# Clustered attention and a maxout FFN: small operations on other engines, weight chains by threes, other weight layout, new order

## The chip, the cores and the metric

The kernel runs on one core of a Trainium2 chip. A core has a matrix engine (TensorE, PE in the profile, with its weight loads as PEld), VectorE (DVE), ScalarE (ACT), GpSimd (POOL) and SyncE (SP), which here only issues DMA. Each engine works through its own list of instructions in order and waits on semaphores for the others. The metric is the device time of one execution in microseconds.

## The reference

Four batches, eight heads, 768 tokens, 64 values per head, 16 centroids per head. Each query and each key goes to the centroid with which its cosine is largest, and a query sees only keys of its own cluster:

```python
mask = q_assign[:, :, :, None] == k_assign[:, :, None, :]
scores = np.where(mask, scale * q @ k.T, -1e9)
attn = exp(scores - max(scores)) ; attn /= sum(attn) + 1e-9
x = (attn @ v), heads side by side            # 3072 x 512
h = max(max(x @ w1, x @ w2), x @ w3)          # 3072 x 768
out = h @ w_out                               # 3072 x 512
```

All inputs and the output are float32.

## The kernel before

*Precision.* TensorE works mostly on pairs of float16 values: each float32 operand is scaled by a power of two and split into a high half and a low half (what the high half leaves), and a product is three float16 products. The power of two comes from a maximum over the tile (L736, L738 for queries and keys), a little matmul that spreads the maxima over the partitions (L754, L407), and a few operations on one or two columns.

*Preparation* (`prep`). Heads go in pairs, four pairs per batch. For each pair the transposed queries and keys are loaded (L730; pair 0 to 3 of batch 0 share four buffers, so the loads of pair 2 wait until pair 0's two tiles have been read by the low-half operation L809), scaled and split, multiplied with the centroids (`cluster_raw`, L787 and L796 in batch 0, on float32), and the winning cluster is turned into one-hot rows ("mask rows") that are added to the contraction of the score matmuls, so that keys of other clusters come out far below. The first pair of batch 0 is "fast": its copies between partition halves (L852) and its four mask rows (L653) are done by compute engines and not by DMA.

*Attention* (`visit`, `tile_units`). A visit is one batch, one pair and one half of the queries: six score tiles of 128 queries by 768 keys, in time order 192 steps. Each tile: score matmuls into PSUM (L1288, L1290; three large PSUM buffers in all), a scaling with the maximum (L1299, VectorE), the exponential with its sum (L1305, ScalarE). From batch 1 on ("norm") the sum is scaled (L1325) and inverted (L1326) on VectorE, and the tile is multiplied with it while it is split (L1363 or L1361, then high half L375 to L377, then low half L1311 or L1372). On even steps from 24 on the exponentials stay in their PSUM buffer until the low half is taken. Tiles are transposed by TensorE (L1336) in the even steps below 40 and in the first pass of batch 0, by DMA (L1314) otherwise. At the end of a visit the product with the values (L1225 or L1236) gives a part of x.

*Weights* (`weights`, `piece`, `split16`). Each of 18 input weight pieces (w1, w2, w3 by six blocks of 128 columns) is loaded (L1032), converted from float32 bits by a cast (L1037 or L1039) and a shift-and-or (L1043), scaled and split. The six row blocks of w_out go the same way, and each has a chain of its own on VectorE: row maximum (L1107), floor, cut to a power of two, reciprocal, factor.

*FFN* (`ffn`). For each of eight groups of 384 tokens 18 hidden products (L1453, twelve matmuls each), their maximum in PSUM evictions (L1467), a split, and three output products (L1508, eighteen matmuls each), an eviction (L375 or L377) and a store (L1522).

*What sets the order.* The kernel is a list of "units" (one operation each, with what it depends on and the buffers it leases), numbered as they are added. `ORDER` says in which order they are emitted, and so each engine's program order; `HANDS` gives, for each unit that several engines could do, one letter: V VectorE, S ScalarE, G GpSimd, Q SyncE. A buffer is leased by the next unit in the order that needs one.

Of the kernel before, what the change touches and what calls it, by code (L numbers as in the profile page):

```python
# [41 lines left out]
1110 319 1114 1123 1099 1124 1125 1117 1129 313 1066 314 1118 1119 1130 1135 232-235 1120 1131 317 249 1115 250  # L42
# [7 lines left out]
2594 2595 344 427 1183 1218 453 336 2592 1148 345 454 1207 1219 2596 290 295 1203 1197 296 346-348 337 2597 455  # L50
# [14 lines left out]
545 2635 1312 1341 1346 546 1347 520 1313 448 1360 1369 2641 550 2685 1353 1370 1354 1371 575 1355-1357 2642 521  # L65
2645 547-549 576 522 1358 577 1361 551 2643 1314 484 1359 1348 2646 2644 2647 2648 523 2649 1362 552 553 524
1377 554 555 1349 2650 1372 578 485 1373 579 580 486 487 1378 1374 2651 581 1379 527 526 525 528 1332 488-490
584 1375 1363 2686 1380 1364 585 1381 2653 556 557 1350 2652 561 586 558 1342 1397 2654 1398 1365 1333 2655 491
1389 1366 1367 1334 1382 1399 2656 2657 562 1406 563 1390 2661 1414 588 1351 1368 559 1400 1407 1383 2658 2662
2659 564 1384 565 1376 633 560 2663 1385 1415 566-568 1391 1392 1408 1416 2660 1417 569 2665 2664 1401 2666 573  # L70
1409 1393 1418 492 1402 582 1419 1394 493 1410 1411 1395 571 572 1423 2671 2669 1424 1412 2670 2667 1403 1404
1431 1396 1420 1421 1386 1432 1425-1427 2668 2672 1428 1433 1387 1434 1429 1435 1436 570 1413 1388 2673 1443
# [14 lines left out]
2726 644-646 1635 1667 1668 618-620 1646 683 649 621 667 712 1636 684 1637 1638 2727 1603 1604 2728 685 1651 686  # L87
# [154 lines left out]
def kernel(  # L242
    ctx: ExitStack,
    tc: tile.TileContext,
    qk: bass.AP,
    vv: bass.AP,
    cent: bass.AP,
    w1: bass.AP,
    w2: bass.AP,
    w3: bass.AP,  # L250
    w_out: bass.AP,
    out: bass.AP,
):
    nc = tc.nc
# [1320 lines left out]
```

## Time and profile before

| | us |
|---|---|
| median of 3 runs | 696.37 (696.34 to 697.27) |
| the profiled execution | 696.72 |
| its span, first to last instruction | 694.9 |
| TensorE busy | 669.1 |
| VectorE busy | 584.4 |
| ScalarE busy | 463.1 |
| GpSimd busy | 408.8 |

The span is what the profiler saw between the first and the last instruction; the execution's own time has some start and end around it. Busy times are sums over the whole span, so an engine may be full in one stretch and idle in another. The mean granted clock of TensorE is 0.985 of full speed.

### The profile page before, as it was taken

The page shows a single profiled execution, that of the slowest core. Times are in us where ns is not written, and L with a number is a line of the kernel's source. Part 1 is how long each engine was busy: PE and PEld are TensorE (multiplying, and loading weights), DVE is VectorE, ACT ScalarE, POOL GpSimd, SP SyncE. Part 2 cuts the span into 40 slices and gives each one's busy share as a digit, 9 for nine tenths or more (in the row PEclk, how much of TensorE's full clock was granted, in tenths as well). Part 3 has the DMA queues.
Part 4 walks back from the last instruction along what each step waited for, and adds up shares of the span by engine and source line. Part 5 has one row for each costly group of instructions (what it writes and reads, how often), then busy time and mean ns, then how long its engine had stood idle before and what let it go on. Part 6 is the DMA issues. An engine that isn't in the chain of part 4 may idle for free. (4 is left out here: it accounts for less than half of the span.)

```text
span 694.9 us, 13112 instructions
## 1 busy us (share of the span) xinstructions
PE 669.1 (96%) x4529; PEld 389.3 (56%) x4529; DVE 584.4 (84%) x1452; ACT 463.1 (67%) x814; POOL 408.8 (59%) x394
## 2 busy tenths in 40 slices
PE   3899989999999999999999999999999999999997
PEld 1666546655555645655556555655555545665563
DVE  7988999999999988999898978899898787885221
ACT  6888999999676567786766558777557656541100
POOL 2478687887765576687676555866874753440010
PEclk8599999999999999999999999999999999999999
DMA  7665458989789999999999989997999898687001
GB/s 245 196 197 164 144 154 237 206 173 200 166 187 200 165 203 181 189 207 177 231 150 196 178 172 218 200 201 163 222 175 189 143 145 144 121 144 122 31 1 45
DMA packets 279553, 117.87 MB, mean 170 GB/s; under 512 B 254272, under 2 KB 265408, under 8 KB 279488
## 3 DMA queue, kind: packets, MB, share of 16 engines
q1 hardware_dynamic: 279488, 117.05, 80.3%
q8 instruction: 35, 0.57, 0.3%
q14 instruction: 30, 0.25, 0.1%
HBM read 33.06 MB, written 6.29 MB: 57 GB/s over the span
## 5 line engine op out<-in xcount | busy, mean ns | idle before, releaser
L1299 DVE TENSOR_SCALAR_CACHE_REDUCE big<-big,nsc 128x768 f32<-128x768 f32 x192 | 192.7, 1018 | 13.7 <-PE big L1290 12.5
L1453 PE MATMUL one<-x,w16a 128*128 128x384 f16 x1152 | 196.5, 326 | 0.4 <-DVE q_p L758 0.4
L1453 PEld LDWEIGHTS <-w16a 128*128 128x128 f16 x1152 | 112.1, 98 | 76.0 <-issue 1.0
L1311 POOL TENSOR_TENSOR e<-e 128x768 f16<-128x768 f32 x77 | 127.2, 1654 | 42.2 <-ACT e L373 31.2
L1305 ACT ACTIVATE e<-big,nm 128x768 f32<-128x768 f32 x116 | 104.5, 902 | 65.8 <-DVE big L1299 40.9
L1288 PE MATMUL big<-qk 128*128 128x512 f16 (+1 forms) x384 | 95.4, 330 | 5.5 <-ACT e L1305 3.9
L1453 PE MATMUL one<-x,w16b 128*128 128x384 f16 x576 | 99.0, 326 | 0.0
L1290 PE MATMUL big<-qk 96*128 96x512 f16 (+1 forms) x384 | 95.4, 329 | 0.0
L1236 PE MATMUL big<-pt,v 128*64 128x384 f16 x1008 | 87.3, 327 | 0.0
L1305 ACT ACTIVATE big<-big,nm 128x768 f32<-128x768 f32 x76 | 66.3, 872 | 21.8 <-DVE big L1299 15.5
L1453 PEld LDWEIGHTS <-w16b 128*128 128x128 f16 x576 | 55.7, 98 | 38.5 <-issue 1.8
L1372 DVE SCALAR_TENSOR_TENSOR e<-big,rs,e 128x768 f16<-128x768 f32 x72 | 72.5, 1011 | 5.4 <-ACT e L375 4.9
L1236 PEld LDWEIGHTS <-v 128*64 128x64 f16 x1008 | 55.8, 110 | 29.2 <-issue 6.8
L375 ACT ACTIVATE e<-big,rs 128x768 f16<-128x768 f32 x55 | 49.4, 899 | 28.6 <-DVE rs L1326 11.6
L1288 PEld LDWEIGHTS <-qk 128*128 128x128 f16 x384 | 34.9, 99 | 36.8 <-issue 15.1
L377 POOL TENSOR_SCALAR e<-e 128x768 f16<-128x768 f32 x38 | 31.6, 833 | 37.6 <-ACT e L1361 15.4
L1290 PEld LDWEIGHTS <-qk 96*128 96x128 f16 x384 | 37.9, 99 | 26.0 <-issue 1.0
L823 POOL TENSOR_TENSOR qk<-stage,qk 128x768 f16<-128x768 f32 x29 | 47.7, 1651 | 8.1 <-ACT qk L373 7.3
L1363 POOL TENSOR_SCALAR e<-e,rs 128x768 f32<-128x768 f32 x31 | 28.4, 917 | 37.1 <-DVE rs L1326 23.7
L1508 PE MATMUL one<-wo,vf_h 128*128 128x512 f16 x216 | 48.4, 379 | 0.0
L1508 PE MATMUL one<-wo,wf_h 128*128 128x512 f16 x216 | 48.3, 379 | 0.0
L1467 DVE SCALAR_TENSOR_TENSOR wf_h<-one,wf_h 128x384 f32<-128x384 f32 x48 | 26.5, 551 | 24.6 <-PE one L1453 24.5
(204 smaller groups left out, 1054.0 us busy)
## 6 DMA issues: line engine op xcount, KB each, us to landing
stage<-in_qk_dram SPq DMA_DIRECT2D x32, 384.0 KB, 4.1
wd<-in_moe_w_dram SPq DMA_DIRECT2D x18, 512.0 KB, 4.0
stage<-in_v_dram SPq DMA_DIRECT2D x16, 384.0 KB, 4.1
out_dram<-o SPq DMA_DIRECT2D x24, 256.0 KB, 3.1
qk<-qk SPq DMA_DIRECT2D x15, 384.0 KB, 4.9
qk<-qk SPq DMA_DIRECT2D x30, 192.0 KB, 3.4
wd<-in_moe_w_out_dram SPq DMA_DIRECT2D x6, 512.0 KB, 4.0
qk<-cl_t SPq DMA_DIRECT2D x60, 48.0 KB, 2.2
```

What stands on the lines that cost most here:

```text
L375: eng.activation(out, x, AF.Copy, scale=k)
L377: eng.tensor_scalar(out, x, k, 1.0, op0=ALU.mult, op1=ALU.mult)
L823: eng.tensor_tensor(t()[:, AQ, i], x(), t()[:, BQ, i], op=ALU.subtract)
L1236: nc.tensor.matmul(t()[D * i : D * i + D, 0:nb], v()[:, i, kt, a], pts[i % len(pts)]()[:, rows[i], c * QT + kt, :], start=(m == 0), stop=( ...
L1288: nc.tensor.matmul(t()[:, lo:hi], aq[:, qs], ak[:, lo:hi], start=True, stop=False)
L1290: nc.tensor.matmul(t()[:, lo:hi], bq[0:K2, qs], bk[0:K2, lo:hi], start=False, stop=True)
L1299: nc.vector.tensor_scalar(s, s, -SCALE if exact else nscs[:, b, pr : pr + 1], 3.0e38, op0=ALU.mult, op1=ALU.min, accum_out=nm())
L1305: nc.scalar.activation(e(), t()[:, 0:S], AF.Exp, bias=nm(), scale=-1.0, accum_out=r)
L1311: eng.tensor_tensor(hv()[:, 1, :], e(), hv()[:, 0, :], op=ALU.subtract)
L1372: eng.scalar_tensor_tensor(hv()[:, 1, :], e(), r(), hv()[:, 0, :], op0=ALU.mult, op1=ALU.subtract)
L1453: nc.tensor.matmul(t()[:, 0:nb], w16[jt // JA][:, jt % JA, wa, i, ct], x16[b, gi, ct]()[:, xa, 0:nb], start=(m == 0), stop=(m == 3 * CT - 1),)
L1508: nc.tensor.matmul(t()[:, 0:DM], h16(jt)[:, ha, tt * P : (tt + 1) * P], wo16[0][:, jt, wa, :], start=(m == 0), stop=(m == 3 * JT - 1),)
```

## The change

The list of units changes in five ways. The four copies of the first pair and its mask rows may also be done by GpSimd, and its two high-half scalings too; the sum scaling of each normalized tile, until now the first of a chain of two on VectorE, becomes a unit of its own that VectorE, GpSimd or ScalarE may do; the four small operations on the row maxima of w_out work on three columns at a time; the input weights come from the host as one array in which each piece is one run of 4 KB per partition; and both lists are new. There are 3041 units instead of 3057. In the new hands the sum scaling goes 56 times to ScalarE, 50 times to GpSimd and 38 times to VectorE; one of the first pair's two high-half scalings goes from ScalarE to VectorE; the copies and mask rows of the first pair stay on ScalarE.

```diff
 ORDER = """
...
-1053 299 168 173 149 1058 150 148 147 300 169 303 1067 1068 1060 211 301 1047 1048 1077 1078 1072 1069 1061 1079
...
+0 3 1 2 4 5 7 19 18 8-15 30 6 21 20 16 17 22 23 51 53 52 54 24 39 25 40 26 27 55 153 28 41 56 57 29 33 177 31 35
...
 HANDS = """
...
@@ mask_rows
-                rows.append(add({"DVE": 0.27, "ACT": 0.84}, 0, row, [u] + moves, [ct, t], base, port=True))
+                rows.append(add({"DVE": 0.27, "ACT": 0.84, "POOL": 0.85}, 0, row, [u] + moves, [ct, t], base, port=True))
@@ prep
-                h = add({"ACT": 0.84, "DVE": 0.53}, 0, hi_s, [u], [x, small, t], base, port=True)
+                h = add({"ACT": 0.84, "DVE": 0.53, "POOL": 0.95}, 0, hi_s, [u], [x, small, t], base, port=True)
...
-            ways = {"ACT": 1.4, "DVE": 0.46}
+            ways = {"ACT": 1.4, "DVE": 0.46, "POOL": 1.6}
@@ piece
-            nc.sync.dma_start(out=x.rearrange("p (a m) -> p a m", a=src[1]), in_=src[0])
+            nc.sync.dma_start(out=x, in_=src)
@@ weights
-                w = (w1, w2, w3)[i].bitcast(I16).rearrange("(c p) n -> p c n", p=P)
-                src = (w[:, :, 4 * jt * P : 4 * (jt + 1) * P], CT)
+                src = w_in[jt, i].bitcast(I16)
...
+            u = piece(w, prio, part, x)
+            parts.append((part, add("DVE", 0.6, rowmax, [u], [x], prio), prio))
+            if jt % 3 != 2:
+                continue
+            s = plan.lease("w_s", lambda i: sb.tile([P, 3], F32, tag=f"w_s.{i}", name="w_s", bufs=1))
+            rows = worow[:, jt - 2 : jt + 1]
...
-                (0.06, lambda row=row: nc.vector.tensor_scalar_max(row, row, 1e-30)),
+                (0.06, lambda rows=rows: nc.vector.tensor_scalar_max(rows, rows, 1e-30)),
                 (0.06, cut),
             ]
-            u_r = plan.chain("DVE", small, [u], (), prio)
+            u_r = plan.chain("DVE", small, [u for _, u, _ in parts], (), prio)
             small = [
-                (0.07, lambda row=row, s=s: nc.vector.reciprocal(s(), row)),
+                (0.07, lambda rows=rows, s=s: nc.vector.reciprocal(s(), rows)),
                 (0.06, lambda s=s: nc.vector.tensor_scalar_mul(s(), s(), 2.0**14)),
             ]
...
+            for i in range(3):
+                part, _, p = parts[i]
...
+                u_wo[jt - 2 + i] = [u_r, split16(part, x, lambda i=i, s=s: s()[:, i : i + 1], s, hi, lo, [u] + u_raw, p)]
+            parts.clear()
@@ tile_units
-            inv = [
-                (0.06, lambda: nc.vector.tensor_scalar(r(), r(), 1.0e-9, 2.0**-14, op0=ALU.add, op1=ALU.mult)),
-                (0.07, lambda: nc.vector.reciprocal(r(), r())),
-            ]
-            u = plan.chain("DVE", inv, [u], [rs], step)
+            def total(eng):
+                if eng is nc.scalar:
+                    eng.activation(r(), r(), AF.Copy, bias=1.0e-9 * 2.0**-14, scale=2.0**-14)
+                else:
+                    eng.tensor_scalar(r(), r(), 1.0e-9, 2.0**-14, op0=ALU.add, op1=ALU.mult)
+            def inv():
+                nc.vector.reciprocal(r(), r())
+            u = add({"DVE": 0.06, "POOL": 0.06, "ACT": 0.12}, 0, total, [u], [rs], step)
+            u = add("DVE", 0.07, inv, [u], [rs], step, tail=0.04)
@@ kernel
+    w_in = np.stack([moe_w1, moe_w2, moe_w3]).reshape(3, -1, 128, moe_w1.shape[1] // 128, 128)
+    w_in = w_in.transpose(3, 0, 2, 1, 4).reshape(moe_w1.shape[1] // 128, 3, 128, -1)
```

In the new order, on VectorE both maxima of the first pair stand behind the copies of the centroids (L497, L500); the scaling that it takes over stands ahead of both L809, and the first weight conversion ahead of the last mask transpose of the first pair. On TensorE the little product L754 of pair 2 and the transposes of two tiles come ahead of the fourth score tile, and the L754 of batch 1's first pair comes behind two score tiles and not ahead of them.

## Rows read from the trace of the kernel before

**Rows 1.** The page, part 1: busy us, share of the span and count by engine.
```profile
PE 669.1 (96%) x4529; PEld 389.3 (56%) x4529; DVE 584.4 (84%) x1452; ACT 463.1 (67%) x814; POOL 408.8 (59%) x394
```

**Rows 2.** Stretches: length, busy PE, PEld, DVE, ACT, POOL, clock, DMA, GB/s.
```profile
0.00:34.00 34.00, 20.47 (x85) 13.16 (x86) 29.09 (x75) 26.36 (x42) 12.78 (x43) 0.70 0.69 222
34.00:80.00 46.00, 45.22 (x332) 28.97 (x329) 41.33 (x89) 40.71 (x78) 32.12 (x31) 1.00 0.63 182
80.00:142.00 62.00, 57.10 (x420) 35.07 (x419) 61.31 (x133) 58.16 (x106) 49.00 (x45) 1.00 0.71 184
142.00:200.00 58.00, 56.58 (x384) 32.01 (x383) 55.66 (x158) 49.79 (x85) 43.34 (x36) 1.00 0.91 186
200.00:640.00 440.00, 438.66 (x3029) 252.02 (x3027) 382.52 (x973) 282.99 (x498) 268.33 (x238) 1.00 0.93 178
```

**Rows 3.** Timeline, TensorE in the head: start, length, instruction, idling before it.
```profile
19.02 4.90 PE L796 MATMUL one<-cwn,stage 128*128 128x32 f32 x22 [1.79 <-DMA stage<-in_qk_dram]
...
28.34 0.80 PE L1288 MATMUL big<-qk 128*128 128x512 f16 x2 [0.57 <-ACT e L1305]
```

**Rows 4.** Timeline of the head: ScalarE, and SyncE with the two loads.
```profile
11.51 1.76 ACT L375 ACTIVATE qk<-stage,q_s 128x768 f16<-128x768 f32 x2 [1.72 <-DVE q_s L767]
...
13.61 1.72 SPq L730 DMA_DIRECT2D stage<-in_qk_dram  x2
...
20.66 3.37 ACT L653 COPY qk<-cl_t 32x768 f16<-32x768 f16 x4
```

**Rows 5.** Timeline, VectorE in the head.
```profile
4.63 0.94 DVE L738 TENSOR_REDUCE q_m<-stage 128x1 f32<-128x768 f32 x1
...
9.27 0.98 DVE L572 STREAM_TRANSPOSE cl_t<-big 128x768 f32<-128x768 f32 x1 [0.65 <-PE big L787]
...
11.39 0.55 DVE L584 TENSOR_TENSOR cl_t<-cl_t,cl_m 128x384 f32<-128x384 f32 x1
...
13.91 1.01 DVE L809 SCALAR_TENSOR_TENSOR qk<-stage,q_s,qk 128x768 f16<-128x768 f32 x1
...
22.53 0.69 DVE L1043 SCALAR_TENSOR_TENSOR wf<-wd,top 128x512 int32<-128x512 int32 x1
```

**Rows 6.** Timeline, TensorE: larger waits behind the head.
```profile
88.90 0.48 PE L1288 MATMUL big<-qk 128*128 128x512 f16 x2 [0.67 <-ACT e L1305]
...
97.41 0.23 PE L754 MATMUL one<-ident,q_m 128*128 128x128 bf16 x1 [1.68 <-DVE q_m L748]
...
554.45 0.49 PE L1288 MATMUL big<-qk 128*128 128x512 f16 x2 [1.03 <-ACT e L1305]
```

**Rows 7.** Groups by line: busy us, mean ns, idling before and its releasers.
```profile
L1453 PE MATMUL one<-x,w16a 128*128 128x384 f16 x1152 | 196.5, 326 | 0.4 <-DVE q_p L758 0.4
...
L1311 POOL TENSOR_TENSOR e<-e 128x768 f16<-128x768 f32 x77 | 127.2, 1654 | 42.2 <-ACT e L373 31.2 <-DVE e L377 7.6 <-DVE so L1494 0.9
...
L1325 DVE TENSOR_SCALAR rs<-rs 128x1 f32<-128x1 f32 x144 | 20.2, 146 | 15.2 <-ACT big L1305 9.5 <-ACT e L1305 4.8
L1043 DVE SCALAR_TENSOR_TENSOR wf<-wd,top 128x512 int32<-128x512 int32 x24 | 20.1, 839 | 0.4 <-DVE w16a L1059 0.4
...
L377 DVE TENSOR_SCALAR e<-e 128x768 f16<-128x768 f32 x9 | 5.0, 555 | 0.2 <-DMA pt<-e 0.2
...
L1204 ACT ACTIVATE rs<-rs 128x6 f32<-128x6 f32 x8 | 1.7, 218 | 0.1
```

**Rows 8.** Timeline, GpSimd: its only 128x1 scaling.
```profile
5.01 0.19 POOL L437 TENSOR_SCALAR kbig<-ksel 128x1 f32<-128x1 f32 x1
```

**Rows 9.** The page, part 6: weight loads, KB each, us to landing.
```profile
wd<-in_moe_w_dram SPq DMA_DIRECT2D x18, 512.0 KB, 4.0
...
wd<-in_moe_w_out_dram SPq DMA_DIRECT2D x6, 512.0 KB, 4.0
```

**Rows 10.** Timeline, VectorE and GpSimd at 89 us.
```profile
89.53 1.65 POOL L1311 TENSOR_TENSOR e<-e 128x768 f16<-128x768 f32 x1
...
89.59 2.14 DVE L1043 SCALAR_TENSOR_TENSOR wf<-wd,top 128x512 int32<-128x512 int32 x1
```

More of the change, by code (lines that the diff above doesn't have):

```diff
@@ new lines @@
+1266-1268 1257 1273 1282 517 1254 486 1283 1274 1275 1258 1243 458 1269 518 2611 1284 1285 2612 459 1244 423 487
+460 519 1255 1219 1286 1287 1276 461 1277 1290 462 488 2615 1256 463 1270 1288 1271 1291 1299 1300 493 1220 494
+1289 464 465 467 520 466 490 1307 521 2613 1292 1259 1308 1272 495 491 424 1260 1301 492 425 1302 426 1261 444
+522 1303 1309 2616 523 1304 1278 427 496 1262-1264 1319 558 428 1293 1294 500 2621 1320 429 1336 2614 1295 1296
+1321 1310 524 1297 1322 1279 1280 2622 1305 1337 430 431 501 432 2623 1306 1298 1281 498 1327 559 1323 2624 1328
@@ new lines @@
+526 497 1338 525 1324 527 1325 528 1339 1340 1329 1311 1312 2618 2619 529 1344 1353 530 560 531 502 503 1345
+1354 2625 1330 1313-1315 468 1341 2626 504 489 532 533 2627 1355 1346 2629 2631 561 505-507 2628 2630 1356 1357
+508 2632 1342 1347 1361 2633 1316 538 1362 535 1358 539 1363 536 537 512 1359 1331 1332 1364 540 541 1348 2634
+2635 469-471 1365 499 509 511 510 562 1366 2637 545 563 564 1343 1360 1326 2636 472 1373 546 547 1381 1349 1333
+2669 473 474 534 568-570 1334 2729 2638 1374 1382 1317 1367 2639 1318 2641 1390 1383 2640 1384 2642 1368 1375
@@ new lines @@
+475 1350 1391 1392 548 1398 2645 2647 542 543 2620 1385 1351 2646 1399 1376 2643 549 1386 1335 2617 1369 1387
+2649 550 544 1400 1393 1394 2644 2648 551 565 476 1401 1388 477 1407 552 553 1352 1377 555 1389 1402 2650 2730
+1408 1378 1395 1379 1396 2651 1409 554 556 2653 1410 2654 2655 2652 557 1411 1412 1415-1417 1370 1403 1418-1420
+1413 1427 1435 1371 1397 1380 1404 2656 1436 1372 1428 1414 1437 1438 1429 2657 2670 2658 1444 1452 1445 1405
+1406 571 2661 1421 1430 2663 1431 1453 1446 2662 2659 2665 1432 1422 1447 1448 1433 1449 1454 1423 1450 2671
@@ new lines @@
+2660 2664 2666 2667 1461 1462 1469 1455 1456 1470 1463 1471 1434 1439 1424 1489 1464-1466 2668 2672 1440 1425
+1472 1467 1490 1491 1473 1492 1451 1441 1442 1481 1426 1457 1506 1498 1493 1474 2673 1458 1494 1459 1507 1499
+1475 1476 2731 1508 1500 2675 616 1468 1443 1482 1483 1515 2674 1516 1517 1460 1477 2678 1501 1484 1485
+1502-1504 1518 1495 1509 1486 566 567 2676 1519 1496 1510 1487 1520 1521 2679 1511 1512 572 1478 1523 1513 1479
+574 573 1480 2677 1524 1543 1535 2681 1488 2685 1522 1525 1497 1536-1538 1544 2682 1526 1539 1527 575-581
@@ new lines @@
+1528-1530 1540 1545 1552 1553 1541 2683 1560 2684 1505 586 587 583 1554 1555 1561 617 1569 1514 2689 2686 1556
+1546 1557 582 1570 1531 1542 588 1562 2687 584 1571 1572 1563 2691 1577 585 1547 1558 1573 1578 1574 1532 1548
+1579 2688 1575 2690 2692 1564 1533 1534 589 1589 1549 1565 1550 1580 618 619 2693 1566 593 594 1590 1591 1606
+1607 1592 1593 1567 1581 2694 1559 662 1576 661 2697 1597 595 1608-1611 2701 1598 1612 2698 1582 2695 2699 2696
+596 597 1594 1599 1551 1568 1614 1613 591 1583 1600 2700 1601 620 1615 1595 1623 1584 598 2702 621 1602 1603
@@ new lines @@
+1585 2680 1596 590 1604 1605 2705 1616 2706 1624 592 1631 622 623 2789 1643 1625 1617 1618 624-626 1632 1644 628
+629 599 600 631 1633 663 1619 601 1645 2703 1626 1627 664 1646 2707 2709 2704 2708 2710 665 1647 1634 1635 666
+1628 1629 1586-1588 1620 1648 1636 632 1649 2715 667 1651 605 668 669 1660 1668 1652 1669 603 602 1637 1661 630
+1621 1630 604 633 2713 1653 1670 1671 670 1638 696 1650 634 2711 1677 2714 1662 638 639 1672 671 676 677 2717
+1685 2712 2716 640 1663 1664 2718 673 641 1654 1678 1665 2721 1686 1679 2790 1666 678 1680 1687 2719 1688 2722
@@ new lines @@
+VSGGSSGSGSGGQQGGVSSGSSGGGSSGQQVGVSVGSSGSGSSGQQGGVSSVSSSGGSVGQQGGVGSGSSGGGGSGQQGGVSSGVSSSGGSGQQGGVSGGSSSSGSSGQQVG
+VSSGSSGSGSGGQQGVVSGGSSSSSSVSGSSSSSSSGGVSSSSVVGVSSVVSSSGGSSGSSGSSGSSGSSGSGGSSGSSGSSGSGGSVGGVSGSVSGSVSGSVSVSVVSSVG
+SGGSSVVSSGVSVSSSGSGSVSSSVSSVGSVGGSVSGSGSGSVSSSGGSVGGSGVSVGSGGSGVVSGGGVSVSSVGVVVSGGGSGSVSSSGGVVSSVGSSVGSGGVGSVVGG
+GVVVSGSGGSVGGSGSSSVSSGGGSVGVGGSSVSSSGSGSVGSGGGSVSSGGGSVGGGGVVSVSGGGVSVSGGGSSVVSGGSVSVGSGGGVVSGSGSSVSGVGSVSVVSSGS
+SVGGGGGSVSGGGVSVVSGSGVSVVGGGVSVSVVGSSSVGGGGGSVSGSVVVVGGSGSSVVVSSGSSVGSGGSSVVSVGSGSVVSSGVSVGSSGGSVGGGGSGSVVGSGSSV
@@ L166 @@
+GSSVGSVSGVGSVSVVGGGSSVGGGGSSVGSVGVSSVGGSVSSVGGGGVVVGGSGSSSVVSSGSSVVGVVVSVSSGGSGSVSSGGGSVVGGGVSVVSSGSGSVGVGGGVVSG
+GGVVVSVVGSGSVSGGGSSVSGSGSSVVSGGSVSVVGGGSSVSGSGGSVVVGGVVVVSGGGSSVSVSGVSVGGGGVSVVSGVVVSGSVVSGSVVSVSVVSVSVVGGSSSSVV
+SGSVVGGSVVGVSVVVGVVVSGSVVGGSVSVVVSVSVVGGSVVGGSVVVGSVVGGSVVGGSSSSVVGVSVVSGSVVSGSVVVVVVVSGSVVGGSVSVVVSVVVVSGSVVSGS
+VVVGVVVSGSVVSGVSSSVVGGVVVSGSVVSGSVVVGSVVGGSVVVVVSVSVVVGVVVVVVVVGGSVVGGVVVSVSVVVVSVSSVVSVSVVVGVVVSVSVVGVSVVGVVVVV
+VSVS
 """
@@ L1028, in piece, with fetch @@
         tl = plan.lease("top", lambda i: top)
-        def load():
+        def fetch():
             x = raw().rearrange("p n w -> p (n w)")[:, 1 : 1 + 4 * n512]
-            nc.sync.dma_start(out=x.rearrange("p (a m) -> p a m", a=src[1]), in_=src[0])
+            nc.sync.dma_start(out=x, in_=src)
         def cast(eng):
@@ L1045, in conv @@
             )
-        u = add("SP", 0.75, load, (), [raw], prio - 2, work=1.95)
+        u = add("SP", 0.75, fetch, (), [raw], prio - 2, work=1.95)
         u = add({"ACT": 0.64, "POOL": 0.7}, 0, cast, [u], [raw, tl], prio)
@@ L1098, in weights @@
             prio = W_0 + W_STEP * (18 + jt)
-            w = w_out.bitcast(I16)[jt * P : (jt + 1) * P, :].rearrange("p (a n) -> p a n", a=1)
+            w = w_out.bitcast(I16)[jt * P : (jt + 1) * P, :]
             part = lambda x=x, i=jt % 3: x()[:, i * n512 : (i + 1) * n512]
-            u = piece((w, 1), prio, part, x)
-            s = plan.lease("w_s", lambda i: sb.tile([P, 1], F32, tag=f"w_s.{i}", name="w_s", bufs=1))
             row = worow[:, jt : jt + 1]
@@ L1107, in rowmax, with cut @@
                 nc.vector.tensor_reduce(row, part(), axis=AX.X, op=ALU.max, apply_absolute_value=True)
-            def cut(row=row):
-                rowi = row.bitcast(I32)
+            u = piece(w, prio, part, x)
[4 more added lines that the diff above has]
+            rows = worow[:, jt - 2 : jt + 1]
+            def cut(rows=rows):
+                rowi = rows.bitcast(I32)
                 nc.vector.tensor_scalar(rowi, rowi, 0x7F800000, None, op0=ALU.bitwise_and)
-            u = add("DVE", 0.6, rowmax, [u], [x], prio)
             small = [
-                (0.06, lambda row=row: nc.vector.tensor_scalar_max(row, row, 1e-30)),
+                (0.06, lambda rows=rows: nc.vector.tensor_scalar_max(rows, rows, 1e-30)),
                 (0.06, cut),
             ]
-            u_r = plan.chain("DVE", small, [u], (), prio)
+            u_r = plan.chain("DVE", small, [u for _, u, _ in parts], (), prio)
             small = [
-                (0.07, lambda row=row, s=s: nc.vector.reciprocal(s(), row)),
+                (0.07, lambda rows=rows, s=s: nc.vector.reciprocal(s(), rows)),
                 (0.06, lambda s=s: nc.vector.tensor_scalar_mul(s(), s(), 2.0**14)),
@@ L1123, in weights @@
             u = plan.chain("DVE", small, [u_r], [s], prio)
-            hi = lambda jt=jt: (w_half(1), wo16[0])[1][:, jt, 0]
-            lo = lambda jt=jt: (w_half(1), wo16[0])[1][:, jt, 1]
-            u_wo[jt] = [u_r, split16(part, x, s, s, hi, lo, [u] + u_raw, prio)]
+            for i in range(3):
+                part, _, p = parts[i]
+                hi = lambda jt=jt, i=i: (w_half(1), wo16[0])[1][:, jt - 2 + i, 0]
+                lo = lambda jt=jt, i=i: (w_half(1), wo16[0])[1][:, jt - 2 + i, 1]
+                u_wo[jt - 2 + i] = [u_r, split16(part, x, lambda i=i, s=s: s()[:, i : i + 1], s, hi, lo, [u] + u_raw, p)]
+            parts.clear()
         prio = W_0 + W_STEP * 24
```

115 lines of the change are left out of this document (40 added, 75 removed), and 125 rows, old and new, of the table ORDER.

## Prediction

> **What bounds the kernel now.** I read the page's busy line first. TensorE is busy for 669.1 of 694.9 us [rows 1]: 25.8 us of idling is all that a change which leaves the matmuls alone can win, unless it also moves time spent at a low clock. Next the busy time by stretches [rows 2] shows where the 25.8 us lie: 13.5 in 0 to 34 us, 0.8 in 34 to 80, 4.9 in 80 to 142, 1.4 in 142 to 200, 1.3 in the 440 us up to 640, and the rest, 3.9, at the end, behind the last matmul. In 80 to 142 us VectorE is busy for 61.3 of 62 us and ScalarE for 58.2, so there the two feeding engines bind. From 200 to 640 us VectorE has 57 us to spare, ScalarE 157, GpSimd 172, and TensorE is the bound. The reader should see that the page's 84% for VectorE is a mean over a stage that has no VectorE time left and one that has plenty.
>
> The timeline of TensorE in the head [rows 3] shows what sets the start. The cluster product of pair 2 (L796) waits for a load until 19.02 us and runs 4.90 us; the first scores are behind it in program order. That load is the second of two that SyncE could issue only from 13.61 us on [rows 4], as each needs the buffer of a tile that L809 on VectorE has read; the second L809 runs from 13.91 us for 1.01 [rows 5]. So the head hangs on VectorE's list up to the second L809. ScalarE's four mask rows (L653, 20.66 + 3.37 = 24.03 us [rows 4]) end just behind the product (23.92) and bind nearly as hard. TensorE works at the lower clock for part of this: the granted clock of 0 to 34 us is 0.70 on the mean [rows 2].
>
> The larger waits behind the head [rows 6] are 1.68 us at 97.41 (a little product on pair maxima of batch 1, whose operand VectorE wrote late), 0.67 at 88.90 and 1.03 at 554.45 (scores waiting for an exponential to free PSUM).
>
> **The change, part by part.** *Sum scalings (L1325).* All 144 ran on VectorE, 146 ns each [rows 7]. By the new list of hands 38 stay, 56 go to ScalarE and 50 to GpSimd. VectorE is relieved of 106 x 0.146 = 15.5 us. ScalarE gets 56 times the nearest row, L1204 with 218 ns: 12.2 us. GpSimd gets 50 times L437's 0.19 us [rows 8]: 9.5 us. The tiles that have them begin with batch 1, and nearly all of this lies in the stretch in which TensorE is busy for 438.7 of 440 us. I take 0: TensorE's queue of hidden and output products covers it. It can't win more than the 1.3 us idle there. If the cover is gone, each scaling on GpSimd lengthens the time for which a score tile holds PSUM (second rival).
>
> *Output weight chains by three rows.* Four small operations for each of six row blocks become four for each of two: 16 fewer, at the 146 ns of L1325 [rows 7] 2.3 us less on VectorE, before batch 1. New wait: the scalings of the first two blocks wait for the third block's row maxima. Behind them in their queues stand other splits; the first reader is the rescaling ahead of the first output product, long after. I count it in the interior term below.
>
> *Input weights in one run per partition.* 18 loads of 512 KB in runs of 1 KB become runs of 4 KB. The six output weight loads are of the same size and already one run, and both kinds land in 4.0 us [rows 9]. I take 0, between 1 us earlier and 1 us later per load, hidden as the two buffers and not the transfers pace these loads.
>
> *Small copies and mask rows of pair 0.* GpSimd is allowed for them, but in the new list all four copies and all four rows stay on ScalarE; only one of the two L375 scalings goes, from ScalarE to VectorE. So nothing of the head goes to GpSimd here.
>
> *Order, head.* The new VectorE order has both maxima after the four centroid copies. Before, one of them (4.63 us, 0.94 long) filled the wait for the transpose that the copies need [rows 5]. Moving it costs some 0.15 us and not 0.94, because VectorE sat idle for 0.65 us before 9.27 until TensorE had the cluster scores [rows 5]; I allow 0.15 for what sticks out past that. Between the L584 at 11.39 and the second L809 the new order adds the scaling (nearest row L377 on VectorE from SBUF, 555 ns [rows 7]) and three tiny operations (0.07 to 0.15 us each), and takes out one reduction of the same 128x384 as L584 (0.55). Net 0.2 to 0.45, I take 0.3. The second load, its landing and the product move by 0.45 us. ScalarE has an L375 (half of 1.76 [rows 4]) and another scaling less ahead of the rows, but the rows now wait for VectorE's last transpose, which has about 1 us more ahead of it, so they end near 24.2 us: no gain. After three score tiles the old list goes on with a fourth, which needed the first exponential and waited 0.57 us until 28.34 [rows 3]; the new one goes on with the little product of pair 2, which needs the second score maximum and a reduction. I set 0.15 for this on top. Head: +0.6 us. Bounds: -1.8 (if the loads don't gate, ScalarE's list decides, two scalings of 0.9 shorter) and +1.5 (the wait at 28.34 is doubled and the fourth tile lost with it).
>
> *Order, 34 to 200 us.* Here 7.1 us of TensorE idling stand. Counted in program order ahead of the first scores of batch 1, ScalarE has 2 large operations less (22 leave, 20 come), some 1.7 us by the 0.84 to 0.88 us of L653 and L375 [rows 4]; VectorE is even but for the sixteen tiny ones. So the waits for exponentials near 88 us should shrink somewhat. In the new TensorE order the little product of 97.41 comes after two score tiles, not ahead of them, and its 1.68 us wait finds cover. VectorE was late for it since a conversion (L1043) took 2.14 us beside a GpSimd subtraction of 1.65 us [rows 10]; all 24 conversions took 20.1 us [rows 7], 3.5 more than 24 times the 0.69 of the one at 22.53 [rows 5]. Where such meetings fall in the new order can't be read from the old trace. I take -2.4 us: the 1.68, and 0.7 for the waits for exponentials (one like that at 88.90). Bounds: -7.1 (all idling goes) and +3.5 (as much again is lost to new meetings).
>
> *End.* The last matmuls, the last eviction on ScalarE and the store are in the same order: 0.
>
> **Sum.** +0.6 - 2.4 = -1.8 us: the span goes from 694.9 to 693.1 us and the profiled execution from 696.7 to 694.9. That execution lies 0.35 us above the median of the runs (696.37), for which I forecast 694.6 us, 0.26% faster. A measurement of this kernel tells some 0.2% (1.4 us) from no change.
>
> **Rivals.** *First: no change, 696.4 us.* The new order removes these waits and makes others of the same size; the head's 0.6 is paid. For it: all waits behind the head are below 1.7 us and scattered, and both orders put nearly the same products at the same places, with feeding engines as full as before (61.3 and 58.2 of 62 us). Against it: the largest wait has a plain cause that the new order takes away.
>
> *Second: slower, 699.0 us.* Of the 50 scalings on GpSimd, 26 belong to tiles whose exponentials stay in PSUM until the low halves are taken, and 19 of the 50 stand directly behind a subtraction of 1.65 us (L1311 [rows 7]) in GpSimd's queue. A scaling caught there comes up to 1.65 us late, and so do the reciprocal on VectorE and the tile's two halves; its PSUM buffer, one of three, is freed later and the scores behind it wait, as at 554.45 [rows 6]. The mean delay is half, 0.8 us; if one in five of the 26 reaches TensorE, 5 x 0.85 = 4.4 us, less the forecast 1.8: 696.4 + 2.6 = 699.0. It decides once the delay exceeds the hidden product (twelve matmuls at 196.5 / 1152 us [rows 7], 2.0 us) that stands between many score tiles. Against it: GpSimd is busy for only 268 of 440 us, and TensorE hardly waited there. [...]
>
> *Third: much faster, 690.6 us.* The head goes by ScalarE's shorter list (-1.8) and more than half of the 7.1 us goes (-4.0). For it: ScalarE's rows ended within 0.1 us of the product. Against it: the loads at 13.61 us waited for VectorE.
>
> **Chances.** Forecast (692.5 to 695.0) 0.37; first rival 0.33; second 0.24; third 0.06. Faster by over 0.2%: 0.43, within 0.2%: 0.33, slower: 0.24. The range goes down to 691.0, just short of the third rival, and up to 699.3, a little past the second.
>
> **What will show it.** Head: the long L796 of pair 2 should start near 19.4 us instead of 19.02, and the scores follow; scores before 23 us are the third rival. Interior: no TensorE wait over 1 us between 80 and 142 us and about 2.5 us of idling there instead of 4.9; if it is 4 us or more, the first rival. From 200 to 640 us TensorE idles under 2.5 us; if it is over 4 and the waits lead back to scalings on GpSimd, the second. It would be wrong altogether if the granted clock in 0 to 34 us moved from 0.70 by more than 0.05, or if weight loads landed at another time than 4.0 us and paced a stage.

## The result: slower by 1.3%, and where

The changed kernel takes 705.62 us at the median against 696.38 before: a ratio of 1.0128, 95% interval 1.0110 to 1.0146. Forecast were 694.6 us; the time is also above the range. The profiled execution took 705.81 us with a span of 704.0, 9.1 us longer than before. The experiments below were timed in four groups, each beside the kernel before, whose median was 695.8 to 696.4 us; a difference between two groups is uncertain by these 0.6 us.

The page's part 1 after (columns as in [rows 1]), and the stretches, which answer to [rows 2]:

```profile
PE 672.5 (96%) x4529; PEld 394.0 (56%) x4529; DVE 579.2 (82%) x1325; ACT 477.1 (68%) x881; POOL 419.0 (60%) x440
```

```profile
0.00:34.00 34.00, 21.03 (x88) 13.31 (x88) 29.05 (x73) 24.28 (x39) 12.51 (x43) 0.80 0.69 231
34.00:80.00 46.00, 45.04 (x329) 28.73 (x328) 41.84 (x94) 40.51 (x76) 33.52 (x33) 1.00 0.55 166
80.00:142.00 62.00, 57.90 (x426) 35.46 (x423) 60.92 (x126) 59.87 (x113) 47.88 (x45) 1.00 0.74 186
142.00:200.00 58.00, 53.03 (x352) 30.56 (x351) 56.19 (x127) 49.20 (x87) 39.63 (x36) 0.97 0.88 177
200.00:640.00 440.00, 435.31 (x2992) 253.21 (x2990) 375.89 (x882) 297.54 (x560) 282.49 (x283) 1.00 0.93 177
```

TensorE's idling is 5.0 us in 142 to 200 us (before 1.4), where the clock also falls, and 4.7 us in 200 to 640 (before 1.3). VectorE is busy for 5.2 us less in all, and the kernel is slower. The timeline of TensorE after, with the waits that answer to [rows 3] (the first) and [rows 6]:

```profile
18.93 5.30 PE L795 MATMUL one<-cwn,stage 128*128 128x32 f32 x24 [3.79 <-DMA stage<-in_qk_dram]
...
87.03 0.49 PE L1293 MATMUL big<-qk 128*128 128x512 f16 x2 [1.29 <-ACT e L1310]
...
133.78 0.49 PE L1293 MATMUL big<-qk 128*128 128x512 f16 x2 [1.02 <-DVE pt L1364]
...
154.68 0.22 PE L406 MATMUL one<-ident,sc_m 128*128 128x128 bf16 x1 [3.73 <-DVE vf_h L1479]
...
524.20 3.09 PE L1241 MATMUL big<-pt,v 128*64 128x384 f16 x35 [1.29 <-DMA pt<-e]
```

The wait of 3.73 us is new, and the product that has it is the little one of the output weights' power of two. The groups by line, answering to [rows 7], and the weight loads, answering to [rows 9]:

```profile
L1316 POOL TENSOR_TENSOR e<-e 128x768 f16<-128x768 f32 x78 | 130.6, 1675 | 42.9 <-ACT e L372 26.8 <-DVE e L376 9.7 <-DVE so L1506 3.8
L1334 POOL TENSOR_SCALAR rs<-rs 128x1 f32<-128x1 f32 x50 | 11.4, 229 | 41.9 <-ACT big L1310 19.0 <-ACT e L1310 15.0 <-ACT rs L1332 3.6
L1332 ACT ACTIVATE rs<-rs 128x1 f32<-128x1 f32 x56 | 10.9, 200 | 0.9
L1123 DVE TENSOR_SCALAR w_s<-w_s 128x3 f32<-128x3 f32 x2 | 2.4, 1200 | 0.0
L1117 DVE TENSOR_SCALAR worow<-worow 128x3 f32<-128x3 f32 x2 | 1.7, 851 | 0.0
L1114 DVE TENSOR_SCALAR worow<-worow 128x3 int32<-128x3 int32 x2 | 1.6, 780 | 0.0
```

```profile
wd<-in_w_in_dram SPq DMA_DIRECT2D x18, 512.0 KB, 4.0
...
wd<-in_moe_w_out_dram SPq DMA_DIRECT2D x6, 512.0 KB, 5.1
```

The last three groups are the news: operations on three numbers per partition with means of 0.78 to 1.20 us. The one-column ones of the kernel before took 0.14 to 0.16 us on the mean.

To say where the 9.1 us lie I matched the instructions of both traces in program order and read when each attention-value product starts. A visit is one batch, head pair and half of the query rows; 32 of them follow each other. Stretches in us, the experiments below beside them:

| stretch | before | after | one column | two columns | scalings by reciprocal | new, then old list | late scalings | all GpSimd scalings |
|---|---|---|---|---|---|---|---|---|
| start to visit 5 | 135.6 | 135.2 | 135.3 | 135.4 | 134.3 | 134.4 | 134.3 | 134.0 |
| visit 5 to 8 | 67.1 | 71.7 | 67.7 | 71.8 | 68.8 | 67.7 | 67.7 | 68.1 |
| visit 8 to 23 | 288.8 | 289.6 | 289.8 | 289.8 | 298.2 | 289.4 | 289.4 | 294.1 |
| visit 23 to 28 | 95.3 | 100.0 | 99.4 | 97.7 | 99.8 | 95.9 | 97.9 | 98.2 |
| visit 28 to 31 | 50.4 | 49.8 | 49.8 | 49.8 | 50.1 | 50.4 | 49.8 | 49.8 |
| visit 31 to end | 57.8 | 57.7 | 57.7 | 57.7 | 57.7 | 57.8 | 57.7 | 57.7 |

So +4.6 us between visits 5 and 8 (135 to 207 us) and +4.7 between visits 23 and 28 (497 to 597 us). The last six columns have one list in the first stretch and still differ by 1.4 us there: that is the scatter of a single profile. Between visits 23 and 28 the kernels after, with one column and with two have the same list and the same engines, and differ by 2.3 us (100.0, 99.4, 97.7): a gain of that size in this stretch is not read from one trace.

### The profile page after: what moved, and what is told of

Same layout as the page of the kernel before. It is cut to its first block, busy times and chain, and to the rows that moved or that the text cites. A ratio compares the mean times of both kernels' runs of the same rounds, so it can differ in the third digit from the quotient of the medians.

```text
span 704.0 us, 13105 instructions
## 1 busy us (share of the span) xinstructions
PE 672.5 (96%) x4529; PEld 394.0 (56%) x4529; DVE 579.2 (82%) x1325; ACT 477.1 (68%) x881; POOL 419.0 (60%) x440
## 4 chain that ended last, share of the span: by engine, by line
PE 66%; DVE 14%; DMA 7%; POOL 4%; ACT 4%; issue 4%; SPq 0%; DVEq 0%; POOLq 0%; ACTq 0%
PE one L1465 29%; PE one L1520 9%; PE big L1241 9%; PE big L1293 6%; PE big L1295 6%; DMA pt<-e 6%; DVE big L1304 4%; PE big L1348 2%; ACT e L1310 2%; PE big L1230 2%; POOL e L1316 2%; DVE wf L1042 1%; POOL e L376 1%; DVE e L1384 1%; PE one L795 1%
## 5 line engine op out<-in xcount | busy, mean ns | idle before, releaser
L1316 POOL TENSOR_TENSOR e<-e 128x768 f16<-128x768 f32 x78 | 130.6, 1675 | 42.9 <-ACT e L372 26.8
L1241 PEld LDWEIGHTS <-v 128*64 128x64 f16 x1008 | 59.5, 110 | 28.5 <-issue 8.9
L374 ACT ACTIVATE e<-big,rs 128x768 f16<-128x768 f32 x60 | 53.4, 897 | 25.3 <-DVE rs L1337 12.8
L1375 POOL TENSOR_SCALAR e<-e,rs 128x768 f32<-128x768 f32 x36 | 33.7, 937 | 28.9 <-DVE rs L1337 21.9
L1479 DVE SCALAR_TENSOR_TENSOR wf_h<-one,wf_h 128x384 f32<-128x384 f32 x48 | 26.4, 549 | 24.9 <-PE one L1465 24.4
```

The costliest lines, as they stand in the source:

```text
L374: eng.activation(out, x, AF.Copy, scale=k)
L1241: nc.tensor.matmul(t()[D * i : D * i + D, 0:nb], v()[:, i, kt, a], pts[i % len(pts)]()[:, rows[i], c * QT + kt, :], start=(m == 0), stop=( ...
L1316: eng.tensor_tensor(hv()[:, 1, :], e(), hv()[:, 0, :], op=ALU.subtract)
```

## The first half: three columns instead of one

VectorE of the changed kernel around the new wait (start, length, instruction), and GpSimd at the same time:

```profile
130.74 0.15 DVE L1117 TENSOR_SCALAR worow<-worow 128x3 f32<-128x3 f32 x1
...
147.51 1.55 DVE L1117 TENSOR_SCALAR worow<-worow 128x3 f32<-128x3 f32 x1
...
149.94 0.73 DVE L1114 TENSOR_SCALAR worow<-worow 128x3 int32<-128x3 int32 x1
...
150.78 0.17 DVE L1122 RECIPROCAL w_s<-worow 128x3 f32<-128x3 f32 x1
...
150.96 1.68 DVE L1160 TENSOR_TENSOR vf_h<-vf_h 128x384 f16<-128x384 f32 x1
152.57 0.14 DVE L390 TENSOR_SCALAR sc_m<-sc_m 128x1 int32<-128x1 int32 x1
152.63 1.53 DVE L1123 TENSOR_SCALAR w_s<-w_s 128x3 f32<-128x3 f32 x1
154.08 0.54 DVE L1479 SCALAR_TENSOR_TENSOR vf_h<-one,vf_h 128x384 f32<-128x384 f32 x1
```

```profile
147.39 3.25 POOL L1316 TENSOR_TENSOR e<-e 128x768 f16<-128x768 f32 x2
150.60 1.63 POOL L909 TENSOR_TENSOR v<-stage,v 128x768 f16<-128x768 f32 x1
152.19 1.95 POOL L822 TENSOR_TENSOR qk<-stage,qk 128x768 f16<-128x768 f32 x1
```

Each long three-column one ends where a GpSimd subtraction ends: 149.06 (the first of the two that take 3.25 together), 150.67 (the second, 150.64), 154.16 (152.19 + 1.95 = 154.14). The first one, at 130.74, met no GpSimd instruction and took 0.15 us: it is the hold that costs, and not the width by itself. The subtraction L1160 on VectorE is held too: 1.68 us, where the seven of the kernel before take 0.55 on the mean. The one-column L390 at 152.57 ran in 0.14 us while GpSimd was busy. VectorE works in order, so the eviction L1479, which frees the PSUM buffer that the little product needs, ends at 154.62, and the product starts at 154.68.

TensorE pays twice. Behind the wait its matmuls are long for a while (start, length): from 155 to 158 us its granted clock is 0.50, and it is 1.00 from 148 us to the wait's end and again from 159 us on:

```profile
156.49 0.85 PE L1295 MATMUL big<-qk 96*128 96x512 f16 x2
157.26 1.36 PE L1219 MATMUL one<-ident,rs 128*64 128x128 f32 x12
...
158.90 0.49 PE L1295 MATMUL big<-qk 96*128 96x512 f16 x2
```

**One column again.** The changed kernel, the same list, but the floor, the cut and the scaling each as three instructions (the cut is shown):

```diff
-    nc.vector.tensor_scalar(rowi, rowi, 0x7F800000, None, op0=ALU.bitwise_and)
+    for k in range(3):
+        rowi = rows[:, k : k + 1].bitcast(I32)
+        nc.vector.tensor_scalar(rowi, rowi, 0x7F800000, None, op0=ALU.bitwise_and)
```

> The changed kernel with the floor, the cut and the scaling of the output weight chains each issued as three instructions of one column instead of one of three columns; order, hands and layout as changed. Theory A (a three-column operation from SBUF to SBUF is held until GpSimd's running subtraction ends, a one-column one is not): each of the 18 instructions takes 0.07 to 0.2 us, the output weights' power-of-two product no longer waits 3.73 us at 154.68 (under 1 us), TensorE does not fall to the lower clock behind it, and the median comes down by 3.5 to 6 us to 700 to 702 us. Rival C (the new order alone makes the wait: the output weights are loaded and converted too late): the wait stays over 2.5 us and the time within 1.5 us of the changed kernel.

Measured: 700.72 us, ratio to before 1.0062 (1.0045 to 1.0080), 4.9 us less than the changed kernel with 12 instructions more. VectorE and TensorE of this run:

```profile
147.59 0.28 DVE L1120 TENSOR_SCALAR worow<-worow 128x1 f32<-128x1 f32 x3
...
148.74 0.23 DVE L1115 TENSOR_SCALAR worow<-worow 128x1 int32<-128x1 int32 x3
...
151.12 0.26 DVE L1125 TENSOR_SCALAR w_s<-w_s 128x1 f32<-128x1 f32 x3
```

```profile
151.90 0.22 PE L406 MATMUL one<-ident,sc_m 128*128 128x128 bf16 x1 [0.88 <-DVE vf_h L1490]
```

Three operations in 0.23 to 0.28 us, beside the same subtractions, and a wait of 0.88 us. From the little product to the hidden product behind the scores 3.07 us pass instead of 4.54. The granted clock is 1.00 from 142 to 200 us. The wait (2.85 less) and the clock (1.47) make 4.3 us; visits 5 to 8 are 4.0 us shorter. Theory A holds, and the new order (rival C) is cleared of this half.

**Stride, and two columns.** Is it that the three numbers lie side by side, or that there is more than one?

```diff
-worow = const([P, JT], F32, "worow")
+worow = const([P, JT, 2], F32, "worow")[:, :, 0]   # w_s likewise
```

> The changed kernel with the three columns kept in one instruction but at a stride of two elements (the row maxima and the scales are every second column of a buffer twice as wide). If what exposes the operations to GpSimd is that their elements lie side by side, they take 0.1 to 0.2 us again and the time comes down as with one column, to 700 to 702 us. If it is the number of columns, they are held for 0.7 to 1.6 us as in the changed kernel, and the time stays at 704 to 706 us. Rival C: stays at 704 to 706 us with short operations.

Measured: 705.5 us (1.0133, 1.0112 to 1.0153), with 1.55, 0.72 and 1.53 us for the same three operations. The stride does nothing. Then one instruction of two columns and one of one:

```diff
-    for k in range(3):
+    for k, n in (0, 2), (2, 1):      # columns k to k + n
```

> The changed kernel with the floor, cut and scaling of the chains issued as one instruction of two columns and one of one column. If the hold begins at more than one column, the two-column instructions that meet a GpSimd operation take 0.5 to 1.6 us while the one-column ones behind them take 0.15, and the wait at 154 us is back (over 2 us, 703 to 706 us). If two columns still go free: 0.15 us each and 699 to 701 us.

Measured: 703.94 us, one run. VectorE (the rows join the two instructions of a pair):

```profile
147.70 1.60 DVE L1120 TENSOR_SCALAR worow<-worow 128x2 f32<-128x2 f32 x2
...
152.82 1.59 DVE L1125 TENSOR_SCALAR w_s<-w_s 128x2 f32<-128x2 f32 x2
```

Each pair is as long as the one instruction of three columns was (1.55, 0.73, 1.53 us), where three of one column took 0.23 to 0.28: two columns are held. The step is from one element per partition to two.

**The old kernel made wide.** The same in the other direction: the kernel before, its order and hands, each chain on three columns of which one counts.

```diff
-    rowi = row.bitcast(I32)
+    rowi = wo3[:, jt : jt + 3].bitcast(I32)   # floor, reciprocal, scaling likewise
```

> The kernel before, order and hands as they are, with the floor, cut, reciprocal and scaling of each output weight row block done on three neighbouring columns instead of one (two of them are the next blocks' or spare, their values are not used from here). Theory A: in the old order too the three-column operations are held while a GpSimd subtraction runs: the cut of block 3, which began 1.58 us ahead of the end of one, takes about 1.7 us instead of 0.15, the floor of block 0 about 0.6; in sum 3 to 6 us more VectorE time between 129 and 155 us, and the time goes up by 2 to 6 us, to 698 to 702 us. Rival C (width does nothing, the new order made the loss): 0.15 us each and 696 us.

Measured: 706.99 us (1.0155, 1.0133 to 1.0178): 11 us lost to wider operations alone, nearly twice the upper end expected. In its trace visits 5 to 8 take 75.7 us instead of 67.1, and the visits from 8 on are as long as before. VectorE and GpSimd, and TensorE's two waits:

```profile
153.86 1.60 DVE L1114 TENSOR_SCALAR worow<-worow 128x3 int32<-128x3 int32 x1
155.50 1.56 DVE L1118 TENSOR_SCALAR worow<-worow 128x3 f32<-128x3 f32 x1
...
157.09 1.08 DVE L1114 TENSOR_SCALAR worow<-worow 128x3 int32<-128x3 int32 x1
```

```profile
153.48 1.96 POOL L912 TENSOR_TENSOR v<-stage,v 128x768 f16<-128x768 f32 x1
155.40 1.63 POOL L1314 TENSOR_TENSOR e<-e 128x768 f16<-128x768 f32 x1
156.99 1.15 POOL L1061 TENSOR_TENSOR wo<-wf,wo 128x512 f16<-128x512 f32 x1
```

```profile
158.68 0.88 PE L1217 MATMUL one<-ident,rs 128*64 128x128 f32 x12 [3.68 <-DVE vf_h L1470]
161.41 0.26 PE L409 MATMUL one<-ident,sc_m 128*128 128x128 bf16 x1 [1.86 <-DVE vf_h L1470]
```

Three such operations stand close together; each ends 0.02 to 0.03 us behind the GpSimd instruction that runs when it comes, and by then the next one has started there. The old trace shows the one-column form in the same place, unharmed: VectorE, then GpSimd of the kernel before.

```profile
150.24 0.15 DVE L1111 TENSOR_SCALAR worow<-worow 128x1 int32<-128x1 int32 x1
150.31 0.14 DVE L1115 TENSOR_SCALAR worow<-worow 128x1 f32<-128x1 f32 x1
```

```profile
150.00 1.83 POOL L1311 TENSOR_TENSOR e<-e 128x768 f16<-128x768 f32 x1 [0.16 <-ACT e L373]
```

## The second half: the late list and the sum scalings

GpSimd of the changed kernel ahead of the wait at 524.20 us: the scalings L1334 stand in a row of long instructions.

```profile
506.27 0.83 POOL L376 TENSOR_SCALAR e<-e 128x768 f16<-128x768 f32 x1
507.18 0.19 POOL L1334 TENSOR_SCALAR rs<-rs 128x1 f32<-128x1 f32 x1
507.45 1.64 POOL L1316 TENSOR_TENSOR e<-e 128x768 f16<-128x768 f32 x1
509.18 0.19 POOL L1334 TENSOR_SCALAR rs<-rs 128x1 f32<-128x1 f32 x1
```

**All scalings back on VectorE, at the new places.** Only letters of the list of hands change, 106 of them, first with the wide chains, then with one column (the change in counts, not the lines themselves):

```diff
- total: V x38, S x56, G x50
+ total: V x144
```

> The changed kernel with all 106 sum scalings that went to GpSimd (50) and ScalarE (56) done on VectorE at the same places of the order; the output weight chains stay three columns wide. Theory B (the scalings on GpSimd and ScalarE are what makes the losses at 516 to 546 and 572 to 589 us, as they stand in queues behind 1.65 us subtractions): the milestones behind 500 us come 3 to 5 us earlier against the changed kernel, the wait of 1.29 us at 524.20 goes, and the median is 701 to 703 us. Rival C (the order of the score tiles and halves, not the hand of the scaling, makes these losses): within 1 us of the changed kernel, 704.5 to 706.5. In either case the 3.73 us wait at 154.68 stays.

> One-column chains and all sum scalings on VectorE together; order, input weight layout and the other hands as changed. Theories A and B together: their gains add, 695 to 699 us, so near the kernel before. A alone: as the run with one column, 700 to 702. Rival C: 703 to 706.

Measured: 726.17 (1.0442, 1.0423 to 1.0461) and 719.94 us (1.0354, 1.0331 to 1.0377). Both expectations fell: 19 to 21 us more. The new order puts a scaling close behind its exponential, where only its own engine waits for it. On VectorE everything queues behind it. The waits of VectorE between 200 and 490 us in the first of the two (us in total, times, longest), 1.5 us in all in the changed kernel:

```profile
DVE rs L1334 <- ACT e L1310: 7.1, 9, 1.9
DVE rs L1334 <- ACT big L1310: 3.3, 3, 1.1
```

These waits are a part of the cost and not all of it, as the next run shows.

**Scalings ahead of their reciprocals,** where the old code has them, with one-column chains:

```diff
 def total(eng):
-    ...
+    pass
 def inv():
+    nc.vector.tensor_scalar(r(), r(), 1.0e-9, 2.0**-14, op0=ALU.add, op1=ALU.mult)
     nc.vector.reciprocal(r(), r())
```

> The changed kernel with one-column chains, and each of the 144 sum scalings issued on VectorE directly ahead of its reciprocal, where the kernel before has it (the earlier run with all scalings on VectorE had them at their new, earlier places, where VectorE waited for each exponential in order). Theory B (the scalings on GpSimd and ScalarE, behind long instructions in these queues, make the losses of 3.4 us between 491 and 600 us that the one-column run still shows against the kernel before): the time comes from 700.7 down to 696 to 698 us and the wait for the transposed halves near 524 us goes. Rival C (the order of tiles and halves there makes it): 700 to 702 us. Rival D (VectorE has no room for 106 more tiny operations): 702 to 706 us.

Measured: 709.63 us (1.0198, 1.0175 to 1.0221). Theory B fell as stated: off GpSimd and ScalarE the scalings cost 8.9 us more than the one-column run, above every range stated, 8.5 of them between visits 8 and 23. VectorE's waits of the kind above are 3.1 us here and not 10.4, and yet visits 8 to 23 are as long as in that run (298.2 and 297.9 us). So in the new order the scalings are better off VectorE; against the old list, which has all of them on VectorE and takes 288.8 us there, it is no gain. What makes the 8.5 us was not traced: VectorE is busy for 269 of 298 us there, for 253 of 290 with one column, and for 260 of 289 in the kernel before.

**Only those on GpSimd,** the late 13 (tiles from 144 on), then all 50:

```diff
+    if eng is nc.gpsimd and step >= 144:   # 0 for all
+        moved.append(1)                    # inv() then does the scaling first
```

> One-column chains; of the tiles from 144 on the 13 sum scalings that went to GpSimd are done on VectorE directly ahead of the reciprocal, all else as changed. Second rival of the prediction (scalings caught behind GpSimd subtractions of 1.65 us delay halves and so the late products): visit 23 to visit 28 is 2 to 3.5 us shorter than the 99.4 us of the run with one column (95.3 in the kernel before), 697 to 698.5 us in all. If the scalings are not the cause: 99 to 100 us, and 700 to 702 us.

> The same for all 50 scalings on GpSimd; the 56 on ScalarE stay. If scalings on GpSimd delay work throughout: 696 to 699 us. If they relieve VectorE where it is short (as the 9 us lost with all 106 back on VectorE suggest): 702 to 706 us, with the loss between visits 8 and 22. If neither, 700 to 702.

Measured: 698.69 us (1.0045, 1.0031 to 1.0060) and 706.86 us (1.0155, 1.0134 to 1.0176; its profile is of the shortest run, 703.65 us). Visits 23 to 28 get 1.6 and 1.3 us shorter than with one column, less than the 2 us expected, and visits 8 to 23 4.3 us longer when all are moved. The 4.3 us are clear: kernels with one list and the same engines there differ by less than 0.7 us (289.1 to 289.8), so in the middle the scalings on GpSimd pay. The late gain is not shown to be theirs. The two-column run has all its scalings where the one-column run has them, and takes 97.7 us there without any of them moved. Its product of visit 24 starts without the wait of 1.29 us that the changed kernel has at 524.20:

```profile
522.70 3.12 PE L1252 MATMUL big<-pt,v 128*64 128x384 f16 x36
```

So this wait comes and goes from run to run, and the second rival's mechanism is neither shown nor excluded in the late stretch.

**The late list as a whole.** One-column chains and the changed list up to visit 23, the old order and hands behind; and the other way round on the old kernel (in words; the edit is the list itself):

```diff
+ order = new[:new.index("V23.av")] + [u for u in old if u not in those]
```

> The changed kernel with one-column chains up to the product of visit 23 (492 us), and from there on the order and hands of the kernel before, sum scalings on VectorE beside their reciprocals. If what is left of the loss is made by the late stretch of the new list (order or hands), the stretch from 492 us to the end is as long as in the kernel before (203.5 us from the start of visit 23's product), and the time is 697 to 698.5 us. If it is made by something earlier that stays (buffers further behind, the input weight layout), 700 to 702 us.

> The kernel before up to the product of visit 23 (491 us), and from there on the order and hands of the changed kernel, with the 50 and 56 kinds of scalings on GpSimd and ScalarE that fall there. If the late stretch of the new list costs by itself: 699.5 to 701 us, with a wait for transposed halves at about 523 us. If the loss needs what came before it in the changed kernel: 696 to 697 us.

Measured: 697.22 us (1.0017, 1.0005 to 1.0030) and 700.45 us (1.0069, 1.0050 to 1.0088). The late part of the new list costs 3.5 us against the one-column run and 4.7 against the old kernel, by itself; visits 23 to 28 take 95.9 us in the first and 99.0 in the second. Its order or its engines? One kernel has the new order with the old engines for 78 late units, the other the old order with the new engines (scalings on VectorE):

```diff
+ order = new, hands = {**new, **old_from_v23}
+ order = new_to_v23 + old, hands = new
```

> One-column chains, the changed order throughout, but from visit 23's product on (492 us) each small copy, scaling, high and low half on the engine that it had in the kernel before (78 of them change), the sum scalings as changed. If the new distribution of the late halves among the engines is what still costs, 697 to 698.5 us, as the run with the old late stretch (697.2). If the new late order costs, whatever the hands, 700 to 702 us. If order and hands only fit each other, over 702 us.

> One-column chains, the changed list up to visit 23, then the order of the kernel before with the engines of the changed one (sum scalings on VectorE). If the late order is the cost: 697 to 698.5 us. If the late hands are: 700 to 702 us. If order and hands only fit each other: over 702 us.

Measured: 709.86 (1.0202, 1.0177 to 1.0227) and 712.95 us (1.0240, 1.0218 to 1.0262). Each crossed pair is worse than either list: order and hands only fit each other, and the loss can't be split between them. So the late list, order and hands together, makes the second half of the loss; which part of it does so was not found.

**A version meant to beat both.** Traces with the new list were 0.5 to 1.4 us ahead early, so it was joined to the old one earlier, at visit 6, then 9:

```diff
- new.index("V23.av")
+ new.index("V6.av")     # then V9.av
```

> A version meant to beat both: one-column chains, the changed order and hands up to the product of visit 6 (159 us), where the traces of the earlier runs were 0.5 to 1.4 us ahead of the kernel before, and from there on the order and hands of the kernel before, with its sum scalings on VectorE. If the lead is kept: 695 to 695.6 us. If the two lists don't join without a stall, or the lead is only the scatter of runs: 696 to 698 us.

> One-column chains, the changed list to the product of visit 9 (226 us), then order and engines of the kernel before. The run that joined at visit 23 was 0.7 us ahead at visit 9. Lead kept: 695.2 to 696 us, which is not told from the kernel before. A stall at the join, as with visit 6: 697 to 700 us.

Measured: 700.35 us (1.0059, 1.0041 to 1.0077), with a stall of 3.4 us at the join, more than was expected even with a stall, and 696.22 us (1.0008, 0.9997 to 1.0019). The second can't be told from the kernel before; none is faster. The lead was scatter: up to visit 5 the traces with the new list and hands take 133.4 to 135.6 us.

## Why the prediction was wrong

*Output weight chains by three rows.* This is the step that failed first: "16 fewer, at the 146 ns of L1325 [rows 7] 2.3 us less on VectorE". The count is right and the price is wrong. The four operations took 3.6 us in the kernel before (24 instructions), and take 6.0 (8 instructions) after: 2.4 us more. They sit ahead of a product that TensorE's queue waits for, and with the clock this cost 4 to 5 us of the time, the larger half of the loss. I bounded neither side of this edit, because an operation on three numbers looked like one on one number. The trace of before had rows against it, which I did not look for (groups by line):

```profile
L990 DVE TENSOR_SCALAR cv<-vpow,iv 128x4 f32<-128x4 f32 x3 | 1.2, 404 | 0.0
L1136 DVE TENSOR_SCALAR r_o<-worow,sc_s 128x6 f32<-128x6 f32 x1 | 0.5, 516 | 0.0
```

404 and 516 ns on 4 and 6 columns, against 139 to 160 ns on one; the only one of these four that met no GpSimd instruction, at 531.57 us, took 0.22 us, and the other three (0.43, 0.56 and 0.52 us) end 0.02 to 0.04 us behind the GpSimd instruction beside them. I had read one such meeting there [rows 10] and counted meetings for the conversions, not for the chains. The second rival looked at GpSimd's queue and at the scalings, which stay one column wide and take 143 ns on VectorE. In the changed kernel and in the old one made wide the holds of the chains end 0.02 to 0.03 us behind the GpSimd instruction; two columns are held (0.72 to 1.60 us with the one-column instruction behind) and three (0.73 to 1.55), also at a stride of two (0.72 to 1.55), and one is not (0.14). Why the second element makes the difference was not shown.

*Order and hands behind 200 us.* The sum has no term for them: "I take 0" is said of the sum scalings, and the order is counted only up to 200 us and at the end. The late list by itself costs 3.5 to 4.7 us. This is the second step that failed, a term put at nothing without a reason; its cause inside the list stays open.

*Sum scalings.* "I take 0" is near what visits 8 to 23 show against the kernel before (289.8 us with one column, 288.8 before), but not for the reason given: in the new order the scalings are not covered, and cost 8.9 us when they stand beside the reciprocal on VectorE. The second rival's 699.0 us is near the one-column run. That is luck as far as the runs show: its sign, over 4 us of idling from 200 to 640 us, came true with 4.7, but its other half, waits that lead back to scalings on GpSimd, is not shown.

*Order, 34 to 200 us.* The 1.68 us wait [rows 6] did go, and the stretch from 80 to 142 us idles 4.1 us instead of 4.9, not 2.5: waits of 1.29 at 87.03 and 1.02 at 133.78 came in, as the first rival says. I counted on 2.4 us, and 0.4 are there at visit 5, which is within the scatter of that stretch.

*Order, head.* The second low-half operation (L808, before L809) came 0.37 us later (14.28 for 13.91 [rows 5]), as counted, but the load behind it landed in time: the product starts at 18.93, not 19.4 (before 19.02 [rows 3]), runs 0.4 us longer (in the kernel before, two of its 24 matmuls had already run at 16.63 us), and the first visit's product is 0.2 us late for a forecast of 0.6. The granted clock went from 0.70 to 0.80 [rows 2], past the bound that I set; but the run with the old list up to visit 23 has 0.80 too, and the one with all GpSimd scalings moved, with the new list, 1.00, so it tells nothing of the change.

*Weight layout* and *end:* the 18 input weight loads land in 4.0 us as before [rows 9], as forecast. The six output weight loads, whose layout is the same, land in 5.1 us instead of 4.0, a sign that I had set; but they don't pace the product that waited: its wait of 3.73 us ends with VectorE's eviction (L1479), and with one column, at the same layout, it is 0.88. No run has the new layout alone; the run joined at visit 9 has it and takes 696.22 us. The last stretch is 57.8 and 57.7 us, as forecast.

## What to carry to other kernels

Before small operations are merged, look at the mean times of the trace's operations of the merged shape, not of the shape that is there: here floor, cut and scaling on one element per partition went free beside GpSimd (0.14 us), and on two or three were held for up to 1.6 us. A stretch of one trace differed by up to 2.3 us between runs with the same list, so a gain of that size needs more than one trace. Where one engine's instructions are held by another's, as VectorE's were here, count how many of them stand between a long queue and the product that TensorE waits for. A written order and its list of engines are one thing; letters changed afterwards cost up to 21 us here.

## What was not expected of the hardware

- A floor, cut or scaling of 128x1 on VectorE takes 0.14 us while GpSimd subtracts; one of 128x3 takes 0.7 to 1.6 us, until GpSimd's instruction ends, and at a stride of two, or of 128x2, as long; with no GpSimd instruction beside it, one of 128x3 takes 0.15. A reciprocal of 128x3 (0.17 us) and a maximum over 128x6 (0.16) in the same place did not wait.
- A wait of 3.7 us on TensorE in the busy interior was followed by some 4 us of long matmuls (0.85 us for two of 128x512, 0.49 at clock 1.00), with a granted clock of 0.50 from 155 to 158 us, which cost another 1.5 us.
